# Two levels of Strassen-Winograd for two of four feature blocks, from the fourth group on

## The chip, the cores and the metric

The kernel runs on one core of one Trainium2 chip. The metric is the time of one execution on the device, in microseconds (us); less is better. Before the change it takes 758.84 us, the median of three runs (758.51 to 759.18). The engines are TensorE (PE; the loading of its weights is listed as PEld), VectorE (DVE), ScalarE (ACT), GpSimd (POOL) and SyncE (SP, which only issues transfers here). All data is fp32.

## The reference, cut to what matters

Linear attention without a softmax, a normalization, and a multiplicative feed-forward network on its result. There are 8 batches with 8 heads, 576 tokens and head dimension 64; in the network there are 4608 tokens (8 x 576), 512 features and 1024 inner features.

```python
kv  = einsum('bhsd,bhse->bhde', k, v)         # per batch and head, 64x64
out = einsum('bhsd,bhde->bhse', q, kv)
x   = out / sqrt(mean(out*out, -1) + 1e-6) * g_norm     # to (4608, 512)
a = x @ w1                                   # 512 -> 1024
b = x @ w2
h = (a * b) @ w3                             # 1024 -> 1024
y = h @ w_out                                # 1024 -> 512
```

## The kernel before, in words

**Folding.** Nothing stands between w3 and w_out, so the kernel multiplies them once at the start (lines L612 and L625) and then computes (a*b) @ (w3 w_out) in one projection per group of tokens. g_norm is folded into w1 and w2.

**Groups.** The tokens are worked in nine groups of 512: the first 512 tokens of each of the batches 0 to 7, and a group made of the 64 left-over tokens of all the batches, which has the number 8. The order is 0 to 6, then 8, then 7. While group T goes through the network, the attention of batch T+1 is done in eight pieces (`steps`), which are called from inside the matrix products (`between`). Each piece is a few short matmuls (kv at L339, the product with q at L415), a norm, or a turn of q or x: the norm is a Square on ACT (L383), a reduction on DVE (L384), a reciprocal (L390) and a multiplication from PSUM (L393). A turn is a copy on POOL that sorts 16-bit halves (L296, L298), a transposing transfer issued by SP (L300), and a second copy on POOL (L310). Batches with an odd number also carry the left-over tokens of two batches (`product_left`, L434).

**Gates.** The 1024 inner features are four blocks p of 256. For each block `gates` computes a and b for it and multiplies them. The product of x with w1 and w2 is written as 2x2 blocks and done by one level of Strassen-Winograd (`winograd`, L646): seven products of four logical matmuls each (128x128 times 128x256; in fp32 one logical matmul is two instructions of PE). The weights' sums s1 to s4 are formed once at the start and stay in SBUF; x's sums t1 to t4 once per group (`combine_x`, L688). ACT copies a product out of PSUM (L659) when its bank is needed, DVE adds (L784) and multiplies a by b (L785; for c21 a copy on ACT, L780, and L781). Then come four sums of the products, for the projection (`sum_ab`, L698 and L699).

**Two levels.** In the last two groups, 8 and 7 (`TWICE`), the blocks 0 and 1 are done together by two levels of Strassen-Winograd in `gates_of_two`: p=2 first, then the two blocks, then p=3. For w1 and for w2 there are seven outer products of seven inner ones each, 49 logical matmuls of 128x128 times 128x128 (L875). PSUM's sums are kept by ACT (L888, L889: 512 and 384 wide), added to by DVE (L893, L894) and finished by DVE (`finish`, L905 to L910). The sums of x's blocks that the second level needs are 28 subtractions of 128x128 on POOL (`sum_x`, L844 to L847), written into the tiles of q, k and v, which are unused by then. The sums of the weights' blocks are formed on DVE during groups 3 and 4 (`prepare_w`, L802 to L804), stored to DRAM (L807), and come back in three loads of 896 KB per group (`load_w`, L822). `replace_a21` forms a fourth sum in place.

**Projection.** `project_twice` multiplies a*b by the folded weights with two levels for every group but the first: 98 logical matmuls (L1075), with seven loads of 896 KB of weights' sums per group (`load_b`).

**What sets the order.** PE, POOL and SP run in the order of the program. DVE and ACT are ordered by a scheduler at build time, and DVE too runs in program order from block p=3 to the end of the projection, and in all of the last two groups from the two-level blocks on (`in_order`). `issue_after` places an operation behind another in that order. [...] five for the products (`ps_mm`) and three for attention (`ps_at`); `gates_of_two` uses two of the latter.

## Time and profile before

| | us |
|---|---|
| median of 3 runs | 758.84 |
| the profiled execution | 758.72 |
| its span | 756.9 |
| PE busy | 749.4 |
| DVE busy | 589.4 |
| ACT busy | 267.0 |
| POOL busy | 164.1 |

A span is the time from the first to the last instruction of the profiled execution. An engine's busy time is that of its computing instructions; waits and the issuing of transfers are not in it. A view of groups of instructions gives how many of one kind there were and the mean duration of one. A view of windows gives the busy time of each engine within a stretch of the span. On PE, the groups start at 315.22 (T=3), 390.66 (T=4), 466.92 (T=5), 542.36 (T=6), 617.09 (T=8) and 685.04 us (T=7); their projections start at 368.77, 445.04, 520.48, 595.21 and, for T=8, 663.15.

### The profile page before, as it was taken

The page shows a single profiled execution, that of the slowest core. Times are in us where ns is not written, and L with a number is a line of the kernel's source. Part 1 is how long each engine was busy: PE and PEld are TensorE (multiplying, and loading weights), DVE is VectorE, ACT ScalarE, POOL GpSimd, SP SyncE. Part 2 cuts the span into 40 slices and gives each one's busy share as a digit, 9 for nine tenths or more (in the row PEclk, how much of TensorE's full clock was granted, in tenths as well). Part 3 has the DMA queues.
Part 4 walks back from the last instruction along what each step waited for, and adds up shares of the span by engine and source line. Part 5 has one row for each costly group of instructions (what it writes and reads, how often), then busy time and mean ns, then how long its engine had stood idle before and what let it go on. Part 6 is the DMA issues. An engine that isn't in the chain of part 4 may idle for free.

```text
span 756.9 us, 14948 instructions
## 1 busy us (share of the span) xinstructions
PE 749.4 (99%) x5903; PEld 657.7 (87%) x5903; DVE 589.4 (78%) x1171; ACT 267.0 (35%) x492; POOL 164.1 (22%) x190
## 2 busy tenths in 40 slices
PE   8999999999999999999999999999999999999998
PEld 5455788888899889988998899889988999999997
DVE  7977999639888568758975897567776778996897
ACT  6777787312322232223222322232223223222321
POOL 0000000322511441144114410431143124006000
PEclk9999999999999999999999999999999999999999
DMA  9996954349997845675767567745743470465244
GB/s 319 344 334 177 273 163 102 85 104 271 336 299 248 225 114 177 223 205 141 218 218 210 155 192 223 208 103 173 224 125 53 150 225 28 146 211 186 87 152 139
DMA packets 146554, 143.20 MB, mean 189 GB/s; under 512 B 86580, under 2 KB 133812, under 8 KB 146484
## 3 DMA queue, kind: packets, MB, share of 16 engines
q1 hardware_dynamic: 144032, 127.82, 58.1%
q10 hardware_dynamic: 2452, 14.42, 5.7%
q8 instruction: 47, 0.77, 0.4%
q14 instruction: 23, 0.19, 0.1%
HBM read 105.78 MB, written 19.14 MB: 165 GB/s over the span
## 4 chain that ended last, share of the span: by engine, by line
PE 97%; DVE 1%; DMA 1%; ACT 1%; issue 0%; SPq 0%; ACTq 0%
PE mm L646 55%; PE mm L1075 23%; PE mm L625 7%; PE mm L875 5%; PE at L339 3%; PE at L415 2%; PE at L612 1%; PE at L875 1%; DMA raw<-in_moe_w_out_dram 1%; PE at L1126 0%; DVE ab L163 0%; PE at L358 0%; PE at L434 0%; DVE chunks L170 0%; SPq L198 0%
## 5 line engine op out<-in xcount | busy, mean ns | idle before, releaser
L646 PE MATMUL mm<-xT,w_sb 128*128 128x256 f32 x720 | 165.2, 380 | 0.0
L646 PEld LDWEIGHTS mm<-xT,w_sb 128*128 128x128 f32 x720 | 136.6, 191 | 18.3 <-issue 0.5
L646 PE MATMUL mm<-xc,ws 128*128 128x256 f32 x512 | 116.2, 380 | 0.0
L646 PEld LDWEIGHTS mm<-xc,ws 128*128 128x128 f32 x512 | 97.3, 190 | 13.7 <-ACT p L659 0.8
L296 POOL COPY xT<-xn 128x1024 uint16<-128x1024 uint16 x26 | 31.2, 1227 | 171.9 <-DVE xn L393 171.9
L784 DVE TENSOR_TENSOR c<-mm,u 128x512 f32<-128x512 f32 x32 | 22.0, 689 | 58.4 <-PE mm L646 58.4
L659 ACT COPY u<-mm 128x512 f32<-128x512 f32 x58 | 34.0, 585 | 93.4 <-PE mm L646 82.8
L659 ACT COPY p<-mm 128x512 f32<-128x512 f32 x66 | 38.7, 586 | 73.9 <-PE mm L646 68.5
L646 PE MATMUL mm<-xc,w_sb 128*128 128x256 f32 x256 | 61.4, 383 | 0.0
L625 PE MATMUL mm<-chunks,ab 128*128 128x512 f32 x128 | 60.1, 603 | 1.0 <-DVE chunks L173 1.0
L646 PE MATMUL mm<-xT,ws 128*128 128x256 f32 x240 | 57.4, 383 | 0.0
L785 DVE TENSOR_TENSOR ab<-c 128x256 f32<-128x256 f32 x96 | 53.8, 561 | 2.5
L646 PEld LDWEIGHTS mm<-xc,w_sb 128*128 128x128 f32 x256 | 48.0, 190 | 6.9 <-ACT u L659 0.3
L646 PEld LDWEIGHTS mm<-xT,ws 128*128 128x128 f32 x240 | 45.1, 190 | 6.2
L1075 PE MATMUL mm<-w3o_sb,ab 128*128 128x128 f32 x368 | 48.7, 276 | 0.0
L1075 PE MATMUL mm<-w3o_sb,raw 128*128 128x128 f32 x372 | 48.1, 276 | 0.0
L384 DVE TENSOR_REDUCE inv<-sq 128x8 f32<-128x512 f32 (+1 forms) x40 | 23.4, 627 | 30.0 <-ACT sq L383 30.0
L1075 PEld LDWEIGHTS mm<-w3o_sb,ab 128*128 128x128 f32 x368 | 45.4, 192 | 0.5
L780 ACT COPY c<-mm 128x256 f32<-128x256 f32 x32 | 11.9, 372 | 95.4 <-PE mm L646 95.4
L1075 PEld LDWEIGHTS mm<-w3o_sb,raw 128*128 128x128 f32 x372 | 44.8, 192 | 0.0
L1086 ACT COPY u<-mm 128x512 f32<-128x512 f32 x23 | 13.5, 586 | 85.3 <-DVE raw L1099 46.6
L310 POOL COPY xT<-xn 128x1024 uint16<-128x1024 uint16 x26 | 31.6, 1244 | 54.0 <-DMA xn<-xT 54.0
(300 smaller groups left out, 1378.7 us busy)
## 6 DMA issues: line engine op xcount, KB each, us to landing
w3o_sb<-w3o_l SPq DMA_DIRECT2D x18, 896.0 KB, 5.4
raw<-in_moe_w_dram SPq DMA_DIRECT2D x31, 512.0 KB, 7.1
raw<-w3o_l SPq DMA_DIRECT2D x15, 896.0 KB, 4.7
w3o_sb<-w3o_l ACTq DMA_DIRECT2D x14, 896.0 KB, 4.6
k_sb<-in_k_dram SPq DMA_DIRECT2D x32, 256.0 KB, 4.5
v_sb<-in_v_dram SPq DMA_DIRECT2D x32, 256.0 KB, 4.7
q_sb<-in_q_dram SPq DMA_DIRECT2D x32, 256.0 KB, 3.3
out_dram<-raw SPq DMA_DIRECT2D x14, 512.0 KB, 4.3
```

Source lines behind the costliest of these rows:

```text
L296: copy(to, src.rearrange("p a n w -> p w a n"))
L310: copy(words(dst), src)
L339: nc.tensor.matmul(kv_ps[e * D:(e + 1) * D, r - rs[0], :], lhsT=k_sb[:, e, cols] if j < J else kl[:, 2 * r + e, :], rhs=v_sb[:, e, cols] i ...
L384: nc.vector.tensor_reduce(out=inv[:, i], in_=sq.rearrange("p (h d) -> p h d", d=D), axis=AX.X, op=ALU.add)
L415: nc.tensor.matmul(o_ps[l][tokens, n * D:(n + 1) * D], lhsT=qT[r][rows, e, i, tokens], rhs=kv_b[rows, e, r, :], start=True, stop=True,)
L625: nc.tensor.matmul(sums_ps[half][m], lhsT=w3T[half, c][:, m, :], rhs=chunks[:, c, 1, :], start=(c == 0), stop=(c == KF - 1),)
L646: nc.tensor.matmul(ps[:, u, :], lhsT=lhsT(a_name, u, c), rhs=rhs(b_name, c),  start=(u == 0 and c == 0 and to is None), stop=(c == chunks ...
L659: copies.setdefault(name, []).append(nc.scalar.copy(t, ps))
L784: adds.setdefault(name, []).append(nc.vector.tensor_add(c, one, two))
L785: nc.vector.tensor_mul(dst, c[:, 0, :], c[:, 1, :])
L875: nc.tensor.matmul(ps[place // 4][:, place % 4, :], lhsT=x, rhs=y, start=new and place // 4 not in seen, stop=True, skip_group_check=True,)
L1075: nc.tensor.matmul(to[:, i, :], lhsT=x[:, c, :], rhs=y[:, c, :], start=new and place // 4 not in seen, stop=(c == 1), skip_group_check=True,)
```

## The change

Groups 3 to 6 now also do p=2, then blocks 0 and 1 in two levels, then p=3, as groups 8 and 7 do (`IN_TWO`). All six of them do it in a new form:

- x's sums for the second level move from POOL to DVE: eight subtractions, four 512 wide and four 384 wide, placed behind the addition of c22 in p=2. They are written into `ws0` and `ws1` (the places of the weights' sums s1, s2 and s4 of blocks 0 and 1) and a new tile `xs`.
- The products that need those outer sums of the weights read them from DRAM too. 66 blocks of 64 KB come in five loads per group (four of 896 KB, one of 640 KB) instead of three. Three are issued in the projection before, two inside `gates_of_two`; the three first loads for the projection follow them.
- `prepare_w` moves to groups 1 and 2, `replace_a21` to group 2, with 33 stores of 128 KB instead of 21.
- `gates_of_two` uses the five product banks in a new plan, and only the tiles p1, u2 and p5 to keep sums in; `between` is called in it four times, so that attention keeps its eight pieces.
- The squares of the norm have one buffer instead of two. For the batches 4 and up, `product_left` uses two of attention's banks and comes a piece later, as does the turn of the left-over x.

```diff
-                sq = work.tile([P, G], FP32, name="sq")[:, 0:w]
+                sq = work.tile([P, G], FP32, name="sq", bufs=1)[:, 0:w]
...
-            o_ps = [bank(ps_at, "at"), bank(ps_mm, "mm")]
+            o_ps = [bank(ps_at, "at"), bank(*((ps_at, "at") if b > FIRST_OF_TWO else (ps_mm, "mm")))]
...
-            fs[second].append((a.product_left,))
+            fs[5 if b > FIRST_OF_TWO else second].append((a.product_left,))
...
+    for w in range(2):
+        for n, (name, _) in enumerate(PRODUCTS):
+            keys = ("a11", "a12", "a22", "s3") if name in ("s1", "s2", "s4") else ()
+            for key in (*keys, "s1", "s2", "s4"):
+                BLOCKS[w, n, key] = len(BLOCKS)
...
+        whole = xT[T].rearrange("p i j c n -> p (i j) c n"), xc
+        for (t1, t2, t4, t3), x in zip(x_sums, whole):
+            b11, b12, b21, b22 = (x[:, :, c, i * P:(i + 1) * P] for c in range(2) for i in range(2))
+            nc.vector.tensor_sub(t1, b12, b11)
+            nc.vector.tensor_sub(t2, b22, t1)
+            nc.vector.tensor_sub(t3, b22, b12)
+            nc.vector.tensor_sub(t4, b21, t2)
...
+        mm = [bank(ps_mm, "mm").rearrange("p (i n) -> p i n", n=P) for _ in range(5)]
+        plan = [((0, 1), (2, 3), (4, 2)), ((3, 4), (2, 0), (1, 2))]
+        names = [("p1", "u2", "p5", "p1"), ("p5", "p1", "u2", "p5")]
...
+            load(w, n)
+            if n in (2, 5):
+                between()
...
+        def load(w, n):
+            last = max(at for (v, m, _), at in BLOCKS.items() if (v, m) <= (w, n))
+            if last + 1 >= (len(loaded_w) - len(streams) + 1) * IN_PART:
+                load_w()
+            if (w, n) == (1, len(PRODUCTS) - 1):
+                for _ in range(3):
+                    load_b()
...
+            r1, r3, r2 = ([mm[i] for i in pair] for pair in plan[w])
+            of_p1, of_u2, of_p5, of_last = names[w]
+            products(0, w, r1, True)
+            p1 = keep(of_p1, r1)
...
     TWICE = (B, B - 1)
+    IN_TWO = (*range(FIRST_OF_TWO, B - 1), *TWICE)
...
-            if T == B - 2 and p == 2 and not replaced:
+            if T == FIRST_OF_TWO - 1 and p == 2 and not replaced:
...
-        if T in TWICE:
-            once = iter([T])
-            gates(T, 2, lambda: [sum_x(t) for t in islice(once, 1)])
-            run(sum_ab(2))
+        if T in IN_TWO:
+            turns = iter([False, True])
+
+            def between_and_sums():
+                if next(turns):
+                    with tc.issue_after(adds["c22"][-1].ins):
+                        sum_x(T)
+                between()
+
+            p = 2
+            gates(T, p, between_and_sums)
+            run(sum_ab(p))
...
-                    for _ in range({(3, 1): 2, (3, 2): 2, (4, 1): 2, (4, 2): 1}.get((T, p), 0)):
+                    for _ in range({(1, 2): 1, (2, 0): 3, (2, 1): 3}.get((T, p), 0)):
```

## The prediction

> **What bounds the kernel now.** I read the busy shares first, then the waits of TensorE (PE), then busy time stage by stage, then a stretch of instructions where VectorE (DVE) and GpSimd (POOL) meet. From the page and the view of PE's waits:

> ```profile
> PE 749.4 (99%) x5903; PEld 657.7 (87%) x5903; DVE 589.4 (78%) x1171; ACT 267.0 (35%) x492; POOL 164.1 (22%) x190
> PE mm L277 <- POOL ident masks.py:199: 2.0, 1, 2.0
> PE mm L625 <- DVE chunks L173: 1.0, 1, 1.0
> PE at L612 <- DVE chunks L173: 0.8, 1, 0.8
> ```

> PE is busy 99% and its only three waits lie in the start-up. So matmul time taken out of a group shortens the span, and any new wait of PE lengthens it. The windows by stage say how much room the others have. Columns: length, then busy time (and instructions) of PE, PEld, DVE, ACT, POOL, clock, DMA share, GB/s.

> ```profile
> 315.22:368.77 53.55, 53.55 (x434) 47.03 (x433) 37.98 (x71) 15.14 (x33) 20.53 (x19) 1.00 0.68 180
> 542.36:595.21 52.85, 52.85 (x427) 46.19 (x425) 33.81 (x71) 15.06 (x32) 20.90 (x20) 1.00 0.40 97
> 617.09:629.18 12.09, 12.09 (x58) 10.67 (x57) 6.34 (x15) 2.82 (x5) 9.12 (x20) 1.00 0.60 195
> 629.18:651.07 21.89, 21.89 (x198) 21.89 (x197) 18.77 (x42) 8.29 (x16) 4.57 (x10) 1.00 0.23 79
> ```

> The first two are the gates of groups 3 and 6, four blocks in one level beside attention: DVE works 34 to 38 of 53 us and has slack. The third is one block in one level, the fourth two blocks in two levels in group 8, where there is no attention: PE is still solid, but DVE already works 18.8 of 21.9 us, and x's sums are not among it (POOL makes them). This stretch of the timeline shows what attention adds beside the DVE (start, duration, engine):

> ```profile
> 419.56 0.42 DVE L781 TENSOR_TENSOR ab<-c,mm 128x256 f32<-128x256 f32 x1
> 419.90 0.42 DVE L803 TENSOR_TENSOR w3o_sb<-w3o_sb,w_sb 128x256 f32<-128x256 f32 x1
> ...
> 420.99 2.64 POOL L310 COPY xT<-xn 128x1024 uint16<-128x1024 uint16 x2 [4.26 <-DMA xn<-xT]
> ...
> 421.36 1.26 DVE L803 TENSOR_TENSOR inner_sums<-inner_sums,ws 128x256 f32<-128x256 f32 x1
> ...
> 422.65 1.26 DVE L804 TENSOR_TENSOR inner_sums<-ws,inner_sums 128x256 f32<-128x256 f32 x1
> ```

> The same subtraction takes 0.42 us alone and 1.26 us when it starts under a POOL copy. It ends just after the copy does. Such copies turn x and q for every group but the last two.

> [...] 1.26 against 0.42 us above, while L781, which reads PSUM, averages 0.414 us and L785, with both inputs in SBUF, averages 0.561. [...] the 384-wide addition of L894 took 546 to 558. [...] weight loads are busy 21.89 of 21.89 us in the two-level stage, against 47.03 of 53.55.

> **The change part by part.**

> *PE.* One block in one level takes 12.09 us, 28 logical matmuls at 0.432 us (third window). Two cost 24.18. Two in two levels took 21.89 (fourth window), 98 at 0.223. Four groups gain 4 x 2.29 = 9.2 us. Attention's pieces stay eight a group, and their matmuls too.

> *DVE work.* Two one-level blocks leave. In their place come twelve additions (6 x 0.69 + 6 x 0.55 = 7.4), eight finishes (1.55 each, 12.4), four products (2.8), the sums of two blocks (2.8), and x's sums, now on DVE (4 x 0.69 + 4 x 0.55 = 5.0). That is 30.4 us in for 10.9 out, +19.5 per group by durations, less where ops overlap. Groups 3 and 4 get back some 4 to 5 us each with the weights' preparation. Against the slack of a whole stage (53.5 - 38 = 15.6 us) this looks nearly affordable, but the work is not spread over the stage: it lies between c12 of p=2 and the third product of p=3. The old p=2 work and the norm stand there too.

> *That stretch.* In the order of the compiled DVE program it holds 72 ops in groups 4 and 6: fifteen 512 wide (10.35), ten of 384 (5.5), 29 of 256 (12.2), eight of 128 (2.3), four reductions (2.7), four norm products at 0.683 (2.7) and two reciprocals (0.4): 36.1 us. An independent op starts about 0.085 before the last one ends (419.56 to 419.90 is 0.34 for a 0.42 op). I take that for 28 of them, -2.4, and get 33.7 us; groups 3 and 5, with the leftovers, have 77 ops and 35.0. PE needs for the same stretch the rest of p=2 (5.18), two pieces of attention (2.45 each, 325.67 to 328.08), 21.89 and two products of p=3 (3.45): 35.4, or 36.0 with leftovers. Of this 0.25 passes before c12's addition starts, and 0.75 lies between a copy and its product. So 34.4 to 35.0 us hold 33.7 to 35.0 of DVE work: the DVE has no margin, and what it loses inside, PE loses.

> *Waits by data in each new group.* Only one buffer for the squares remains, so the second reduction waits for a Square that waits for the first reduction. With x's sums ahead in the queue, the addition to p1 (w=0) ends at about 21.2 us from the group's start; products(3) wants that bank at 20.3. That makes 0.8 us, and 0.1 on the copy before. The third product of p=3 needs the tile that the last-but-one finish gives back: 0.8, or 1.5 with leftovers, plus 0.2 for the leftovers' PSUM bank. Sum 1.7 and 2.6, mean 2.1; 8.6 us for four groups. Bounds 0.9 and 4 per group.

> *Collisions.* In the four gates stages now, 172 DVE ops have two SBUF inputs, and 28 of them started under a POOL copy and lost 19.2 us together, 0.69 each. There were 74 copies, so 38% of them caught one, at a time when such ops filled 0.34 of DVE's time. In the new stretch they fill 22 of 35 us (0.63), and by POOL's queue 12 to 15 copies fall in it. If the catch grew in proportion, 70% would be caught, 8 to 10; the DVE waits for data in places, so I take 0.6, 7.6 to 9, at 0.69: 5.2 to 6.3 us a group. Less what the two waits above already hide I still take 5.8, since a collision ahead of a wait lengthens it. Bounds: 0 (all meet ops that read PSUM, or idle) and 10.

> *Groups 8 and 7.* No attention runs, so the DVE fits. But x's sums now follow c22's addition on DVE instead of standing on POOL, which began them earlier. t4 is done about 13.9 us from the start, and the third matmul of products(0) wants it at 12.5: 1.4 us each, 2.8 together. Bounds 0 and 3.5.

> *Weights' preparation in group 2.* Two bursts of nine ops (9 x 0.42 = 3.8 us each) stand there, and each step reuses three tiles that its stores must have left (1.8 us). The cover is the slack of group 2's gates; I put 2 us, bounds 0 and 5. The twelve stores more are issued by SP (0.33 us each) and hidden.

> *DMA.* Five parts of the sums instead of three, two of them loaded inside the two-level stage. Part 4 stands on SP behind two transposes of x that wait for POOL, which waits for the norm on DVE: issued near 21.9 us, landed 5 to 5.4 later (27.3), wanted at 29.3. A margin of 2 us, 1.2 with collisions: nothing, and up to 3 per group if POOL runs later. The rest replaces loads of the projection's sums in the same queue, and the DMA engines were 0.40 to 0.68 busy.

> *Sum.* -9.2 + 8.6 + 4 x 5.8 + 2.8 + 2 = +27.4; off goes 1 us that waits and collisions share, so +26.4. The profiled execution took 758.72 with a span of 756.9, so 1.8 lie outside; the median of the runs, 758.84, stands 0.1 above it. Span 783.3, time 785.

> **The rivals.** *Likeliest: DVE becomes the bound of the new groups' stages,* 776 to 796 (collisions between 3.7 and 8.5 a group). Chance 0.60.

> *Collisions are mostly absorbed.* The waits by data hold gaps of 1 to 3 us, POOL's copies might fall in them or under ops reading PSUM. For it: 25 of the stretch's 72 ops read PSUM or have one input. Against it: no gap is left between x's sums and the last finish. Waits alone give -9.2 + 8.6 + 2.8 + 2 = +4.2, 763; with half the collisions 775. From 760.4 to 775, chance 0.22.

> *The transfer of part 4 comes late,* or DVE's lateness delays POOL, which delays the transposes, which delay that load: 3 us more per group and its sequel, 796 to 815. Chance 0.08.

> *The other side: faster.* The DVE keeps up, and PE's only new waits are the 0.9 at products(2) and (3): 4 x 0.9 + 2.8 - 9.2 = -2.8, 756. For this the tile of the last finish must be free in time and group 2 must hide its burst. It decides at 2.3 us of waits per new group without groups 8 and 7, about 1.6 with them; undisturbed I count 2.1. Chance 0.06. In between, within 0.2% (1.5 us, about what a measurement here can tell), 0.04. That the change does not do what it says is excluded: its compiled PE program has the 98 matmuls in each of the six groups.

> **How the numbers follow.** 785 is the first case. The range has to leave 0.2 outside: 0.06 + 0.04 below 760, about 0.03 of the second case below 764, and some 0.07 above 799. So 764 to 799; the likeliest case's own range is 776 to 796. Faster 0.06, same 0.04, slower 0.90.

> **What would show it.** Right: PE's waits of the new groups come from DVE tiles (p1, p5, u) and banks, 6 to 10 us a group; DVE nearly solid from c12 of p=2 to p=3 in groups 3 to 6; finishes and x's sums stretched from 0.4 to over 1 us beside POOL copies; the two-level stage of groups 8 and 7 still about 21.9 us after one wait of 1.4. Wrong: new waits under 2.3 us a group, or waits on the streamed weights by DMA, or PE's matmuls of 128 columns spaced wider than 0.223 us when attention runs beside them.

## The result, and the profile after

The changed kernel takes 808.63 us, the median of four runs (806.97 to 809.21), against 758.79 for the kernel before (758.51 to 759.18): a ratio of 1.0653, 95% interval 1.0634 to 1.0671. The forecast of 785 had the sign and the place; the loss is nearly twice what it said, and lies above its range (764 to 799).

From the page of the changed kernel and from the view of PE's waits (total us, times, longest):

```profile
PE 760.4 (94%) x6239; PEld 668.8 (83%) x6239; DVE 679.1 (84%) x1339; ACT 278.0 (34%) x516; POOL 140.2 (17%) x132
PE mm L647 <- ACT p L660: 17.9, 10, 3.3
PE mm L899 <- ACT p L919: 5.6, 4, 3.2
PE mm L1108 <- DVE raw L1066: 4.6, 1, 4.6
PE mm L899 <- DVE p L924: 4.5, 4, 2.1
PE mm L899 <- DVE ws L867: 3.4, 6, 1.2
PE mm L899 <- DMA w3o_sb<-w_l: 2.1, 2, 1.2
```

PE now waits some 40 us, mostly for copies out of PSUM by ACT. Such a copy in turn waits for a tile that DVE has not yet given back, as an example below shows. And something else stands in the first line: PE is busy 760.4 us although its matmul work became less (there are more matmuls, 6239 against 5903, but shorter ones); by the forecast's own count 749.4 - 9.2 = 740.2 would do. PE's windows of the new groups 3 to 6 (columns as before: length, PE busy and so on, granted clock ahead of the last two):

```profile
327.73:409.26 81.53, 75.01 (x714) 69.79 (x713) 72.21 (x146) 22.93 (x49) 20.41 (x19) 1.00 0.72 216
409.26:494.66 85.40, 78.47 (x746) 72.52 (x745) 75.20 (x151) 23.87 (x52) 22.69 (x20) 0.96 0.74 212
494.66:577.80 83.14, 76.58 (x715) 70.72 (x714) 73.64 (x146) 23.03 (x49) 20.75 (x19) 0.98 0.72 211
577.80:663.87 86.07, 77.62 (x707) 72.08 (x705) 75.60 (x150) 22.89 (x48) 21.91 (x20) 0.96 0.55 169
```

These are whole groups, projection included. Before, the same four took 75.44, 76.26, 75.44 and 74.73. The granted clock, 1.00 in all of them before, is now 0.96 to 1.00. Set side by side by the starts of the groups, the 50.5 us between the spans (807.4 and 756.9) are these:

| stretch | before | after | more |
|---|---|---|---|
| up to group 2 | 238.72 | 247.16 | 8.4 |
| group 2 | 76.50 | 80.57 | 4.1 |
| groups 3 to 6 | 301.87 | 336.14 | 34.3 |
| group 8 | 67.95 | 69.89 | 1.9 |
| group 7 to the end | 71.86 | 73.64 | 1.8 |

In groups 3 to 6 PE idles 28.5 us (length less busy time in the windows) where it idled 0.1, and is busy 307.7 us where 301.7 - 4 x 2.29 = 292.6 would do: 15.1 more. So the 34.3 are -9.2 of matmuls, +28.4 of waits and +15.1 of slower PE.

Where a wait comes from is best seen at the end of group 4's two-level stage (timeline; start, duration, engine):

```profile
455.78 1.89 PE L647 MATMUL mm<-xc,ws 128*128 128x256 f32 x8
...
458.73 2.48 POOL L311 COPY xT<-xn 128x1024 uint16<-128x1024 uint16 x2 [1.89 <-DMA xn<-xT]
...
460.12 1.37 DVE L937 TENSOR_TENSOR p<-p 128x256 f32<-128x256 f32 x1
460.28 0.59 ACT L660 COPY p<-mm 128x512 f32<-128x512 f32 x1 [2.23 <-DVE c L939]
460.92 3.78 PE L647 MATMUL mm<-xc,ws 128*128 128x256 f32 x8 [3.26 <-ACT p L660]
...
461.41 1.52 DVE L941 TENSOR_TENSOR ab<-ab,c 128x512 f32<-128x512 f32 x1
...
464.50 3.26 PE L647 MATMUL mm<-xT,ws 128*128 128x256 f32 x8
```

POOL's copies hold DVE's finishes (1.37 us for an operation of 0.42), ACT's copy waits for the tile that a finish reads, and PE waits 3.26 us for ACT. Then the eight matmuls take 3.78 and the next eight 3.26 us; undisturbed, eight take 1.89, as in the first line.

An instruction of DVE with two SBUF inputs that took over 0.1 us more than is usual for its form is called caught here. In the four gates stages 28 were caught and lost 19.2 us before, 56 and 41.3 us after, with the same 74 POOL copies. Of the instructions that read PSUM there, 18 of 68 started under a POOL copy before and 21 of 92 after, and none took over 0.01 us more than is usual for its form.

### The profile page after: what moved, and what is told of

Its sections match the earlier page's. It is cut to its first block, busy times and chain, and to the rows that moved or that the text cites. A ratio compares the mean times of both kernels' runs of the same rounds, so it can differ in the third digit from the quotient of the medians.

```text
span 807.4 us, 15838 instructions
## 1 busy us (share of the span) xinstructions
PE 760.4 (94%) x6239; PEld 668.8 (83%) x6239; DVE 679.1 (84%) x1339; ACT 278.0 (34%) x516; POOL 140.2 (17%) x132
## 5 line engine op out<-in xcount | busy, mean ns | idle before, releaser
L647 PE MATMUL mm<-xT,w_sb 128*128 128x256 f32 x528 | 122.4, 382 | 0.0
L647 PEld LDWEIGHTS mm<-xT,w_sb 128*128 128x128 f32 x528 | 100.5, 192 | 13.9 <-issue 0.5
L647 PE MATMUL mm<-xc,ws 128*128 128x256 f32 x384 | 92.5, 393 | 13.5 <-ACT p L660 13.5
L647 PEld LDWEIGHTS mm<-xc,ws 128*128 128x128 f32 x384 | 74.3, 195 | 26.9 <-ACT p L660 16.7
L297 POOL COPY xT<-xn 128x1024 uint16<-128x1024 uint16 x26 | 29.6, 1167 | 193.2 <-DVE xn L394 193.2
L660 ACT COPY p<-mm 128x512 f32<-128x512 f32 x50 | 29.1, 587 | 69.5 <-DVE c L939 34.2
L785 DVE TENSOR_TENSOR c<-mm,u 128x512 f32<-128x512 f32 x24 | 16.5, 686 | 40.4 <-PE mm L647 40.3
L899 PE MATMUL mm<-ws,w3o_sb 128*128 128x128 f32 x300 | 47.6, 279 | 2.1 <-DMA w3o_sb<-w_l 2.1
L647 PE MATMUL mm<-xT,ws 128*128 128x256 f32 x176 | 45.5, 405 | 4.2 <-ACT p L660 4.1
L647 PE MATMUL mm<-xc,w_sb 128*128 128x256 f32 x192 | 46.2, 383 | 0.0
L919 ACT COPY p<-mm 128x512 f32<-128x512 f32 x36 | 21.2, 588 | 63.7 <-PE mm L899 50.5
L899 PEld LDWEIGHTS mm<-ws,w3o_sb 128*128 128x128 f32 x300 | 40.6, 195 | 2.5 <-DMA w3o_sb<-w_l 2.5
L626 PEld LDWEIGHTS mm<-chunks,ab 128*128 128x128 f32 x128 | 21.8, 190 | 24.1 <-issue 15.3
```

The source lines that it names most:

```text
L297: copy(to, src.rearrange("p a n w -> p w a n"))
L626: nc.tensor.matmul(sums_ps[half][m], lhsT=w3T[half, c][:, m, :], rhs=chunks[:, c, 1, :], start=(c == 0), stop=(c == KF - 1),)
L647: nc.tensor.matmul(ps[:, u, :], lhsT=lhsT(a_name, u, c), rhs=rhs(b_name, c),  start=(u == 0 and c == 0 and to is None), stop=(c == chunks ...
L660: copies.setdefault(name, []).append(nc.scalar.copy(t, ps))
L785: adds.setdefault(name, []).append(nc.vector.tensor_add(c, one, two))
L899: nc.tensor.matmul(ps[place // 4][:, place % 4, :], lhsT=x, rhs=y, start=new and place // 4 not in seen, stop=True, skip_group_check=True,)
```

## The experiments

**Is the loss of groups 3 to 6 made inside them?** Two levels for the last two groups alone, all else as changed.

```diff
-    IN_TWO = (*range(FIRST_OF_TWO, B - 1), *TWICE)
+    IN_TWO = TWICE
```

> The changed kernel, but only groups 8 and 7 take the two-level form (groups 3 to 6 do their four blocks in one level as before; the preparation of the weights' sums stays in groups 1 and 2, so groups 3 to 6 compute with a replaced block and only their time is meant). Between the starts of the groups the changed kernel lost 6.1, 9.1, 7.7 and 11.3 us in groups 3 to 6 (34.3 together), 12.5 before group 3 and 3.7 after group 8. Theory (the loss of groups 3 to 6 is made by the two-level stage inside them): 808.6 - 34.3 = 774, within 2. Rival (part of it comes from what is shared, the single buffer of squares, or the later piece of the leftovers, which stay): 778 to 790.

775.78 us (ratio 1.0215, 1.0185 to 1.0245). Groups 3 to 6 took 75.44, 76.70, 75.44 and 74.95: back at the lengths of before. So 33 us belong to the two-level stages beside attention, and the other 17 to what is shared: the preparation, the single buffer, and the new form of groups 8 and 7.

**POOL's reads.** POOL works at the same places and fills the same tiles, but each copy is replaced by a copy of one column and an instruction that only writes:

```diff
+    def write_only(to, src):
...
+        nc.gpsimd.tensor_copy(words, src[:, 0:1, 0:1])
+        nc.gpsimd.memset(to, 0)
...
-    def x_by_dma(h, copy=nc.gpsimd.tensor_copy):
+    def x_by_dma(h, copy=write_only if b > FIRST_OF_TWO else nc.gpsimd.tensor_copy):
```

> The changed kernel, but the POOL copies that turn q and x for the batches 4 to 7 read one column and then only write (zeros) to the same place, so these batches get no attention result; everything else is issued as before. Theory (DVE instructions with two SBUF inputs wait for POOL copies that read SBUF; in the gates of groups 3 to 6, 56 of them lost 41 us): the stretched instructions return to 0.42 to 0.7 us, the waits of these groups fall from 28 us to 4 to 12, the lowered clock after them mostly goes, and the time is 772 to 785. Rival 1 (DVE has too much work even undisturbed): 795 to 805. Rival 2 (PE waits for the streamed weights or for banks whatever DVE does): 803 to 809.

788.22 us (1.0379, 1.0349 to 1.0409), 20.4 less. Not one of the 268 instructions with two SBUF inputs in these gates was caught any more, beside 70 POOL instructions that only write, nearly all of 0.95 us. That is the theory's mechanism, but the time missed its interval by 3 us. PE's waits say why:

```profile
PE mm L904 <- DMA w3o_sb<-w_l: 11.5, 4, 6.2
PE mm L652 <- ACT p L665: 6.5, 9, 2.3
```

With DVE free, a second chain comes to light: the streamed weights' sums. The instructions that only write are also a little shorter than the copies (means of 1.1 to 1.3 us); what that alone would give was not tried.

**x's sums.** Left out in groups 4, 5 and 6:

```diff
-                    with tc.issue_after(adds["c22"][-1].ins):
-                        sum_x(T)
+                    if T not in (4, 5, 6):
+                        with tc.issue_after(adds["c22"][-1].ins):
+                            sum_x(T)
```

> The changed kernel without x's eight subtractions for the second level in groups 4, 5 and 6 (they use those of group 3, so their output is wrong). 4.96 us of DVE work by durations leave each of three groups. Theory (DVE is the bound of the stretch, its loss is PE's loss, and the clock falls after waits): 4 to 6 us a group, 791 to 797. Rival (the waits come from the collisions at the end of the stretch alone, or from transfers; the sums fit into gaps): 804 to 809.

803.74 us (1.0583, 1.0553 to 1.0614): 4.9 less where the theory said 12 to 18. Group 4 even grew, from 85.4 to 89.7. The rival named the transfers, and there they are (timeline of group 4 in this kernel):

```profile
424.40 1.27 DVE L394 TENSOR_TENSOR xn<-at,inv 128x512 f32<-128x512 f32 x2
...
432.63 2.41 POOL L297 COPY xT<-xn 128x1024 uint16<-128x1024 uint16 x2
...
435.07 3.25 SPq L301 DMA_TRANSPOSE xn<-xT  x2
...
438.41 0.54 SPq L845 DMA_DIRECT2D w3o_sb<-w_l  x1
...
443.91 1.22 PE L899 MATMUL mm<-ws,w3o_sb 128*128 128x128 f32 x4 [6.46 <-DMA w3o_sb<-w_l]
```

The norm's last multiplications begin at 424.40, which is 16.5 us after the group's start (407.86); in the changed kernel it is 22.4 (431.62 after 409.26). But POOL's copy of x comes at 432.63, behind the second copies of q, which wait for their own transposes. SP's transposes of x wait for POOL, and the load stands behind them: 30.6 us after the group's start, against 28.6 in the changed kernel. DVE's lateness had hidden this; taking DVE's work away moved the wait.

**The loads past SP's queue.** The two loads inside `gates_of_two` are issued by ACT instead:

```diff
-                load_w()
+                load_w(nc.scalar)
```

> The changed kernel, but the two loads of weights' sums inside the two-level stage are issued by ACT instead of SP, so they no longer stand behind the transposes of q and x. In the changed kernel PE waits 2.1 us for these loads; in the two runs that relieve DVE it waits 11.5 to 12. Theory (two chains run side by side: DVE, and POOL's copies with the transposes and then the load on SP; the second is mostly hidden under the first): only the 2.1 us and what they cause go, 803 to 807. Rival (the late load starts the lateness of the rest): 790 to 799.

807.01 us (1.0640, 1.0607 to 1.0673): 1.6 less, which is not clear of chance. Four of the kernels here (this one, the one with `IN_TWO = TWICE`, and the two without x's sums) have the same program for groups 0 to 2 as the changed one. In the five traces group 2 starts between 247.2 and 248.1 us, and takes 80.6 us in the changed kernel and 78.9 in the others: only there does the clock fall (to 0.50, from 269.15 us on) after the wait of 2.35 us that all five have. The 4.9 us of the run before hold the same 1.7. The late load alone is not the cause of the loss.

Together with POOL's turns that only write:

> Both edits: POOL's turns for the batches 4 to 7 only write (no attention result for them), and the two loads are issued by ACT. The first edit alone gave 788.2 with 11.5 us of waits for these loads, 6.2 the longest. Theory (with both chains free the new groups are as fast as their matmuls plus 1 to 2 us): 770 to 776, no wait for these loads over 1 us. Rival (the loads are late by bandwidth and not by their place in the queue): 783 to 788.

770.82 us (1.0163, 1.0133 to 1.0192), with no wait for a load. The first edit alone gained 20.4, the second alone 1.6, both 37.8: two chains side by side. Groups 3 to 6 then take 74.21, 75.64, 74.20 and 74.33, together 3.5 less than before the change. PE still waits 3.2 us in them by data, without any collision: 0.8 a group, where the forecast had 2.1. Its busy time is 295.2, 2.6 more than 292.6; 2.1 of this are the matmuls around the eight waits, as shown further on. With 3.2 and 2.6 added, the 3.5 are the forecast's 9.2.

And together with x's sums left out:

> Both edits: groups 4 to 6 without x's sums for the second level (their output is wrong), and the two loads issued by ACT. Without the second edit this gave 803.7 with 12 us of waits for the loads. Theory (x's sums load DVE at the front of the stretch, where the late loads hid the gain): the 12 us go, and about 2 of clock: 788 to 793. Rival (the back of the stretch, where the finishes meet POOL's copies, sets the end whatever stands ahead): 799 to 804.

794.71 us (1.0478, 1.0448 to 1.0508), 9.0 less than without x's sums alone. The time lies between the theory's 793 and the rival's 799, which fits with both ends of the stretch counting; the run does not tell them apart.

**The slower PE after a wait.** Artificial waits in the kernel before, where PE hardly waits after the start-up and the clock is 1.00:

```diff
+        if p in (1, 3) and 0 < T < B - 1:
+            last, first = xb[T]["t4"][:, 1, 0:1], xb[T]["b11"][:, 0, 0:1]
+            nc.gpsimd.tensor_copy(last, last)
+            for _ in range(7):
+                nc.gpsimd.tensor_copy(tick, tick)
+            nc.gpsimd.tensor_copy(first, first)
```

`last` is a column that the product before has read, `first` one that the next product reads. This is the shorter form; the longer one stands ahead of p = 2 alone and has 13 copies.

> The kernel before with one artificial wait of PE in each of groups 1 to 6, ahead of block p=2: POOL rewrites a column that the last product has read, does 13 tiny copies one after the other and then rewrites a column that the next product reads. Nothing else changes. Theory (after a wait of about 3 us TensorE's clock is lowered for some us, so a wait costs more than its length): six waits of some 3 us, 18 together, and 6 to 12 us more, granted clock below 0.995: 783 to 791. Rival (the lowered clock in the changed kernel has another cause): the sum of the waits alone, clock 1.00.

The waits came out longer than meant, 7.4 to 12.7 us, since POOL's own copies for attention stood ahead of the chain. They sum to 55.5 us; the time went up by 70.7, to 829.32 (1.0934, 1.0902 to 1.0966). The other 15.2 are 2.5 us for each wait.

> The kernel before with two artificial waits of PE in each of groups 1 to 6, ahead of the blocks p=1 and p=3, with 7 tiny POOL copies each: about 2.5 us a wait instead of the 7.4 to 12.7 of the longer ones, which cost 2.5 us each beyond their length. Theory (waits as long as those of the changed kernel, 2.3 to 3.3 us, lower the clock too, though not each of them): the waits' sum (about 30) and 8 to 20 us more. Rival (it takes longer waits): the sum alone, clock 1.00.

Twelve waits of 2.3 to 5.4 us, 43.4 together; 820.81 us (1.0812, 1.0791 to 1.0834), 61.9 more: 18.5, or 1.5 each, beyond their length. Three of them in the timeline, each with the product after it:

```profile
354.65 1.99 PE L646 MATMUL mm<-xT,w_sb 128*128 128x256 f32 x8 [2.27 <-POOL xT L792]
356.48 3.62 PE L646 MATMUL mm<-xc,ws 128*128 128x256 f32 x16
...
267.56 3.19 PE L646 MATMUL mm<-xT,w_sb 128*128 128x256 f32 x8 [3.02 <-POOL xT L792]
270.54 4.15 PE L646 MATMUL mm<-xc,ws 128*128 128x256 f32 x16
...
614.79 1.99 PE L646 MATMUL mm<-xT,w_sb 128*128 128x256 f32 x8 [3.02 <-POOL xT L792]
616.62 3.62 PE L646 MATMUL mm<-xc,ws 128*128 128x256 f32 x16
```

```profile
264.79:268.20 3.41, 0.64 (x3) 0.59 (x4) 2.09 (x5) 0.36 (x2) 2.35 (x10) 1.00 1.23 192
268.20:271.61 3.41, 3.41 (x10) 2.67 (x9) 0.00 (x0) 0.58 (x1) 2.35 (x3) 0.50 0.92 191
...
609.54:612.95 3.41, 2.23 (x30) 1.60 (x20) 2.31 (x6) 1.99 (x6) 3.41 (x5) 1.00 0.34 76
612.95:616.36 3.41, 1.57 (x7) 1.42 (x8) 1.35 (x3) 0.00 (x0) 3.04 (x10) 1.00 0.75 155
616.36:619.78 3.42, 3.42 (x17) 3.01 (x17) 1.22 (x2) 1.17 (x2) 3.42 (x4) 1.00 0.00 0
```

The first wait fell into one step, in which PE worked 0.64 us; the next step ran at half the clock. The second was cut by the end of a step, PE worked 2.23 and 1.57 us in its two steps, and the clock stayed. Counted over the steps of all the traces that began at full clock (without the first 10 and the last 8 us), 47 in which PE idled more than 1.95 us were all followed by half the clock, none of those with less than 1.86 us (some 3,700) was, and of four in between one was. In the changed kernel alone, six such steps idled 2.08 to 3.41 us and were followed by half the clock; the most idle one that was not, 1.87. So a wait shorter than a step can halve the clock: in the changed kernel one of 2.35 us left 2.08 us of idle time in its step and was followed by 1.7 us of loss.

**The preparation in group 1.**

```diff
-                    for _ in range({(1, 2): 1, (2, 0): 3, (2, 1): 3}.get((T, p), 0)):
+                    for _ in range({(2, 0): 4, (2, 1): 3}.get((T, p), 0)):
```

> The changed kernel, but the one step of the weights' preparation that stands in group 1 moves to group 2, which then does 4 and 3 steps. Group 1 took 82.1 us, 6.5 more than before: one wait of 4.6 us for a sum of the projection that waits for three stores, which stand in SP's queue behind transposes, and a lowered clock after it. Theory (the stores queued on SP hold the tile that the projection's first sum needs): group 1 back at about 75.6, group 2 up by 0 to 2: 802 to 804. Rival (whichever group has the step pays the same): 807 to 810.

804.08 us (1.0588, 1.0557 to 1.0619), 4.5 less, and group 2 starts 6.2 us earlier. In the changed kernel this is what stood there:

```profile
214.21 5.32 SPq L301 DMA_TRANSPOSE xn<-xT  x1
...
219.63 2.61 SPq L301 DMA_TRANSPOSE q_sb<-qT  x2
...
222.33 1.58 SPq L814 DMA_DIRECT2D w_l<-raw  x3
224.52 0.43 DVE L1066 TENSOR_TENSOR raw<-ab 128x256 f32<-128x256 f32 x1 [5.98 <-DMA w_l<-raw]
```

The three stores of that one step stand on SP behind the transposes of x and q. Those of x alone hold SP for 10.15 us, from 209.39 on; POOL's copy of x had ended at 207.81, so they do not wait for it. In the kernel before they hold SP as long (10.26 us), but these stores do not stand behind them. What makes them long was not tried; the view of windows gives the DMA engines as fully busy there (share 1.12). The projection's first sum needs the stores' tile, DVE idles 5.98 us, PE 4.58, and the granted clock falls to 0.50 (for one step of 3.41 us, from 224.78 on). Moving the step away gave the theory's result, 802 to 804, within 0.1. Group 2 still starts 2.2 us later than before the change.

**One buffer for the squares**, in the kernel before, nothing else:

```diff
-                sq = work.tile([P, G], FP32, name="sq")[:, 0:w]
+                sq = work.tile([P, G], FP32, name="sq", bufs=1)[:, 0:w]
```

> The kernel before with one buffer for the squares of the norm instead of two, nothing else. Group 0 of the changed kernel took 1.9 us longer, with a wait of 0.8 us for a copy of ACT. Theory (ACT, waiting for the first reduction with its second Square, empties PSUM late): 759.5 to 761. Rival (no wait of PE follows from it outside the new groups): 758.2 to 759.2.

763.41 us (1.0055, 1.0039 to 1.0072): 4.5 more, above the theory's 761. Nearly all comes before group 2, which starts 3.9 us later.

**Cutting POOL's copies.** If a POOL copy holds up DVE until that one instruction is done, its length should matter. The loads are issued by ACT here too.

```diff
+    def in_quarters(to, src):
...
+        for i in range(4):
+            cut = slice(i * n // 4, (i + 1) * n // 4)
...
+                nc.gpsimd.tensor_copy(to[..., cut], src[..., cut])
```

> The changed kernel with the loads issued by ACT (807.0 so), and each POOL copy of the turns of the batches 4 to 7 cut into four copies of a quarter. Same bytes, same engine. Theory ([...] a DVE instruction waits for a quarter and slips in between, but is caught more often): a caught instruction loses about 0.3 us instead of 0.74, 796 to 804. Rival (what counts is how long POOL reads in all): 806 to 814.

788.22 us (1.0383, 1.0352 to 1.0414), the middle of two runs that lie 3.6 apart: 18.8 less than with whole copies, better than the theory's 796. Now 112 instructions are caught, but they lose 22.3 us in all, 0.20 each, instead of 37.5 us among 52 with whole copies. In the timeline DVE and POOL alternate:

```profile
372.65 0.61 DVE L948 TENSOR_TENSOR c<-p 128x256 f32<-128x256 f32 x1
...
372.93 2.99 POOL L318 COPY qT<-q_sb 128x256 uint16<-128x256 uint16 x5
373.19 0.61 DVE L946 TENSOR_TENSOR p<-p 128x256 f32<-128x256 f32 x1
...
373.72 0.88 DVE L950 TENSOR_TENSOR ab<-ab,c 128x512 f32<-128x512 f32 x1
```

**Can it be mended?** The loads by ACT, the preparation in group 2, x's sums of groups 8 and 7 placed ahead, and the first copy of each turn of the batches 4 to 7 on ACT (`nc.scalar.copy`):

```diff
-                copy(to, words(src).rearrange("p n w -> p w n"))
+                copy_apart(to, words(src).rearrange("p n w -> p w n"))
```

> The changed kernel with four mends, its result complete: the weights' preparation in group 2 alone (this gave -4.5 us), the two loads issued by ACT (-1.6), x's sums of groups 8 and 7 placed ahead (each waits 1.2 us there now), and the first copy of each turn of the batches 4 to 7 on ACT instead of POOL, so that half of POOL's copies are gone from groups 3 to 6. Theory (PE's loss there is DVE's loss to POOL's copies): the collisions' 41 us fall to about 20, 10 to 14 us with the clock, so 784 to 792. Rival (ACT, whose copies empty PSUM, is now late instead): 796 to 803.

787.30 us (1.0367, 1.0347 to 1.0387). 17 are caught and lose 14.2 us. The sums of groups 8 and 7 gained nothing here: moved further ahead, they delayed the end of the projection before, where PE now waits 1.3 and 1.1 us.

Then the copies left on POOL are cut into quarters, and the sums of groups 8 and 7 come later than that:

```diff
-                    with tc.issue_after(adds["c22"][-1].ins):
+                    with tc.issue_after(adds["c12" if T in TWICE else "c22"][-1].ins):
```

> The mended kernel (787.3), its result complete, with the copies left on POOL cut into quarters (uncut they still caught 17 instructions of DVE, 14 us), and x's sums of groups 8 and 7 placed behind c12's addition. Theory (what is left of the new groups' loss is still collisions): 14 us lost fall to 6, 4 to 8 us; groups 8 and 7 up to 3 us: 776 to 783. Rival (ACT, with the copies moved to it, is what PE waits for now): 783 to 788.

776.74 us (1.0225, 1.0148 to 1.0301). 45 are caught now, but lose 9.5 us. The gates of groups 8 and 7 are now 46.57 us, against 48.01 in the changed kernel and 46.06 before.

Last, two buffers for the squares, in bf16 so that they fit:

```diff
-                sq = work.tile([P, G], FP32, name="sq", bufs=1)[:, 0:w]
+                sq = work.tile([P, G], mybir.dt.bfloat16, name="sq")[:, 0:w]
```

> mended_quarters, and the squares of the norm kept in bf16, so that two of them fit in the room of one (their rounding enters the result). Theory (the second Square no longer waits on ACT for DVE's reduction with copies out of PSUM behind it, which cost 4.5 us in the kernel before alone): 4 to 8 us below mended_quarters. Rival (with the other waits gone the Square has time): within 1.5 us of it.

771.75 us (1.0159, 1.0115 to 1.0203): 5.0 less, though the two runs without it lie 2.7 apart. The reductions that read the squares take as long as with fp32 (0.68 us), so the gain is the second buffer's: about what the single buffer costs in the kernel before.

And the same with no copy on ACT:

> mended_squares, but both copies of each turn on POOL in quarters and none on ACT. Theory (ACT has room, POOL's copies are what costs, 0.2 us for each of some 28 caught a group): 3 to 8 us above mended_squares. Rival (copies on ACT ahead of those that empty PSUM cost as much): within 2 us of it or below.

772.21 us (1.0165, 1.0121 to 1.0209), within 0.5: once POOL's copies are short, moving half of them to ACT is worth nothing. No version beats the kernel before: the best stays 12 us above it, 5.4 of them in group 2, where the preparation now stands, and 6.5 in groups 3 to 6, where PE still waits for copies out of PSUM. What would win these back was not tried.

## Why the prediction was right and wrong

**The matmuls' gain, right.** Without collisions and late loads the new groups are 3.5 us shorter than before, after 3.2 us of waits and 2.6 of slower PE: 9.2 within rounding.

**The waits in the new groups, right in sum, partly by luck.** The forecast put 8.6 for waits by data and 23.2 for collisions, less 1, together 30.8 us. PE idled 28.5. By the runs the first part is 3.2, so collisions and late loads make about 25. The wait for the bank of the fourth product, 0.9 in the forecast, is 0.1; the one in p=3 is 0.4 or 1.0, for 0.8 and 1.5. The collisions themselves were counted too low: in the stretch of the forecast 11 to 15 instructions a group were caught, for 7.6 to 9, and DVE lost 9.4 us a group there, for 5.8. Not all of it reached PE.

**The case of absorbed collisions, refuted** by the write-only run: 20.4 us hang on POOL's reading alone, 37.8 with the loads out of the way.

**The transfer of part 4, mis-sized and mis-read.** The forecast had it issued 21.9 us after the group's start, with a margin of 2 us. In groups 3 to 6 it was issued 27.9 to 29.6 us after the start. The step left out that POOL's copy of x stands behind the second copies of q, with the leftovers' copy in groups of odd batches. It cost only 2.1 us of waits in the changed kernel, because DVE was as late. So the measured 808.63 lies in the range of the rival that named this transfer (796 to 815) by chance and not for its reason.

**"A wait costs its length", wrong.** This is the first step that failed, and it was not even written down: every wait entered the sum as it stood, and PE's matmuls at the duration they had before. They became slower, 15.1 us in the new groups. There are two parts. At half the clock, six stretches, each begun by a wait, lost 1.6 to 3.2 us, 11.7 together; four of them, 8.4 us, lie in groups 3 to 6. And every wait, at full clock too, makes the last matmul before it count 0.16 us more than usual in PE's busy time and the first one after it 0.10 (256 wide: the last one counts its whole 0.379 us where the next would start after 0.216, and the first one takes 0.483 for 0.379). Group 3 shows this alone: its clock stays at 1.00, it has seven waits, and PE is busy 1.9 us more than 73.15. In the four groups it is 5.9 us for 24 waits; 0.8 are left. The two runs with artificial waits show that a wait makes the slow stretch. The whole term takes the forecast from 785 to 800. The forecast did name matmuls that are spaced wider as a sign of being wrong.

**The preparation, wrong in place and size.** This is the second step that failed. The forecast costed two bursts in group 2 at 2 us and called the stores hidden. Groups 0 to 2 lost 12.5: 6.5 in group 1, where one step's stores stood in SP's queue ahead of a tile that the projection needs; 4.1 in group 2; 1.9 up to group 1. The last part is the single buffer of the squares: alone in the kernel before, it makes group 1 start 2.4 us later. It was costed in the new groups alone, but costs 4.5 us where nothing else is changed, and acts in the first groups. With the step moved and two buffers of squares, group 2 starts at 238.85, against 238.72 before the change. With this term 10.5 too low, the slower PE of 15.1 missing, groups 8 and 7 0.9 too low and the waits 2.4 too high, the error of 24 is complete.

**Groups 8 and 7, right in mechanism:** each waits 1.18 us for x's sums and 0.21 for a copy, the 1.4 of the forecast, 3.7 with the rest.

## What to carry to other kernels

A wait on the engine that sets the end costs more than its length: here some 0.27 us each, and a stretch of half clock where it leaves PE idle for over some 1.9 us of a step of 3.41 us. A wait of 2 us can do that (one of 1.97 did, in the write-only run); one of twice 1.95, some 3.9 us, must, because one of the two steps that it covers then idles long enough (an estimate from the steps counted above). Sum waits with both. Where instructions of two engines hold each other up, as those of DVE and POOL do here (in the changed kernel a finish of 0.42 us took 1.37, and a POOL copy of 1.15 us up to 2.63), short instructions on the one that is not the bound free the other: cutting copies into quarters gained 18.8 us with no work removed. And before calling a transfer hidden, walk its whole queue, with what each entry ahead waits for: the store or the load at the end inherits all of it.

## What the runs showed that was not expected

- Whether a wait of PE of 2 to 3 us halves the clock is decided by where it falls in steps of 3.41 us: one of 3.02 us did not, one of 2.35 us did, and lost 1.7 us. All waits of 4.6 us and above did, and lost 1.6 to 3.1 us in the changed kernel and the two with artificial waits.
- POOL instructions that only write (70, nearly all of 0.95 us) did not hold up a single DVE instruction.
- One missing buffer of 2 KB per partition on an engine that is busy 35% cost 4.5 us of 759.
